# Linear attention and a two-layer network on one core: attention by head pairs, its divisor spread through DRAM, dense chunks of 512 tokens with attention pieces placed by hand

## The chip, the cores and the metric

The kernel runs on one core of a Trainium2 chip. The metric is the device time of one execution in microseconds (us), the median of several runs. A separate execution was taken by the profiler; its rows are what this document reads.

## The reference

```python
q, k, v: (8, 8, 576, 64)            # batch, heads, tokens, head size
phi = lambda x: np.where(x > 0, x, np.exp(x) - 1.0) + 1.0
q_p, k_p = phi(q), phi(k)
kv = np.einsum('bhsd,bhse->bhde', k_p, v)
z = np.sum(k_p, axis=2)
num = np.einsum('bhsd,bhde->bhse', q_p, kv)
den = np.einsum('bhsd,bhd->bhs', q_p, z)[..., None] + 1e-06
x = (num / den).transpose(0, 2, 1, 3).reshape(4608, 512)
h = x @ w_in                        # w_in: (512, 2048)
out = (h - np.tanh(h)) @ w_out      # w_out: (2048, 512)
```

## The kernel before, in words

A batch is 576 tokens, handled as four tiles of 128 tokens and one of 64, with tokens on the partitions. For each batch GpSimd queues the loads of q, k and v by token tile (they cast f32 to bf16 on the way, lines 96 to 98), behind the two weight loads that stand at the start of the program. `phi` makes each tile in three ScalarE steps (relu, exp, relu) and an addition on VectorE.

Then comes a loop over the eight heads. TensorE sums `kvz_ps` over the five tiles (line 114; column 65 of v is one, so it also sums k) and transposes q into `qTp` (line 117), which VectorE copies into `qT`. For each token tile TensorE makes `nd_ps`, numerator and divisor side by side (line 125); VectorE takes the reciprocal of the divisor, one value for each token, that is for each partition (line 127); ScalarE scales the numerator by it into `res` (line 129); TensorE transposes `res` into `resT` (line 131), and VectorE copies that into `xT_sb`, the feature-major input of the dense layers (line 132). The four PSUM tiles of attention have one buffer each.

After its heads a batch goes through `moe_chunk` twice, for 512 and for 64 tokens. The first layer makes `hps` for 128 of the 2048 features at a time, four matmuls each (line 72); ScalarE takes the tanh, VectorE the difference `gT` (lines 76, 77). The second layer makes `ops` for 128 tokens, 16 matmuls of 512 columns (line 82); VectorE copies it to `osb`, and SyncE writes it out.

The order of the instructions on each engine is decided by a scheduler, which takes from several heads and from both layers by priority; each engine then runs its own queue in order, and waits at an instruction until the tiles that it needs are there.

## Time and profile before

| | |
|---|---|
| median of 3 runs | 747.39 us (745.71 to 749.91) |
| the profiled execution, span from first to last instruction | 748.1 us |
| TensorE matmul busy | 556.6 us, 74% of the span, 2944 matmuls |
| VectorE, ScalarE busy | 346.5 us, 321.6 us |
| mean granted TensorE clock | 0.776 |

The page gives the profiled execution by its span alone; no time outside the span is known for it. Busy times of different engines overlap, so they don't add up to the span. The granted clock is given as a share of 2.4 GHz; the records know the levels 0.5 and 1.0 only, and a mean between them is a mixture. For the first 140 us or so the rows show 1.00 also where matmuls took the time of the lower level, so there the duration of matmuls is the better sign.

### The profile page before, as it was taken

To read this page: it belongs to the slowest core of one execution; us is meant where nothing else is said; L and a number is where in the kernel's file an instruction comes from. 1 tells how busy PE (TensorE), PEld (TensorE's weight loads), DVE (VectorE), ACT (ScalarE), POOL (GpSimd) and SP (SyncE) were. 2 spreads that over 40 slices of the span, in tenths; PEclk is the share of its full clock that TensorE was granted. 3 is DMA by queue.
4 is the path that set the end of the run, shared out by engine and by line. 5 is a ranking of instruction groups with operands and counts; after the bars stand their busy time and mean duration, and the time that the engine had idled before them with its cause. 6 is when DMAs were issued, how large, how long until landed. Compare 5 with 4: busy or idle time off the path is not lost.

```text
span 748.1 us, 9055 instructions
## 1 busy us (share of the span) xinstructions
PE 556.6 (74%) x2944; PEld 270.7 (36%) x2944; DVE 346.5 (46%) x1400; ACT 321.6 (43%) x817; POOL 107.6 (14%) x168
## 2 busy tenths in 40 slices
PE   0065689856997579965898569985699668985697
...
PEclk9999999855797559955698557975599656985599
...
DMA packets 120400, 28.38 MB, mean 38 GB/s; under 512 B 113184, under 2 KB 115232, under 8 KB 120352
## 3 DMA queue, kind: packets, MB, share of 16 engines
...
## 4 chain that ended last, share of the span: by engine, by line
PE 45%; issue 27%; ACT 10%; DVE 9%; DMA 4%; POOL 3%; POOLq 0%; ACTq 0%; DVEq 0%
PE hps L72 16%; PE ops L82 15%; PE resT L131 5%; PE qTp L117 4%; ACT res L129 4%; DMA v<-in_v_dram 4%; DVE xT_sb L132 3%; DVE rden L127 3%; PE kvz_ps L114 3%; ACT tmp L62 2%; ACT tmp L63 2%; DVE qT L118 2%; ACT qa L64 2%; PE nd_ps L125 2%; POOL v L98 1%
## 5 line engine op out<-in xcount | busy, mean ns | idle before, releaser
L72 PE MATMUL hps<-xT_sb,w_in_sb 128*128 128x64 bf16 (+1 forms) x1024 | 186.7, 314 | 7.0 <-DVE gT L77 3.1
L76 ACT ACTIVATE th<-hps 128x512 f32<-128x512 f32 (+1 forms) x256 | 103.8, 412 | 197.0 <-PE hps L72 187.5
L129 ACT ACTIVATE res<-nd_ps,rden 128x64 bf16<-128x64 f32 (+1 forms) x320 | 99.7, 311 | 198.7 <-DVE rden L127 198.5
L82 PE MATMUL ops<-w_out_sb,gT 128*128 128x512 bf16 (+1 forms) x640 | 173.3, 389 | 0.0
L77 DVE TENSOR_TENSOR gT<-hps,th 128x512 bf16<-128x512 f32 (+1 forms) x256 | 115.5, 456 | 105.5 <-ACT th L76 102.0
L131 PE MATMUL resT<-ident,res 128*64 128x128 bf16 (+1 forms) x320 | 92.2, 288 | 78.6 <-ACT res L129 74.8
L117 PE MATMUL qTp<-ident,qp 128*64 128x128 bf16 (+1 forms) x320 | 85.9, 268 | 81.2 <-DVE qT L118 44.4
L132 DVE COPY xT_sb<-resT 64x128 bf16<-64x128 bf16 (+1 forms) x320 | 67.0, 209 | 136.5 <-PE resT L131 133.1
L72 PEld LDWEIGHTS <-w_in_sb 128*128 128x128 bf16 x1024 | 75.1, 100 | 94.5 <-issue 46.4
L131 PEld LDWEIGHTS <-res 128*64 128x64 bf16 (+1 forms) x320 | 39.6, 124 | 170.9 <-ACT res L129 160.8
L98 POOL DMA_DIRECT2D v<-in_v_dram x40 | 33.8, 856 | 449.7 <-PE kvz_ps L114 446.4
L118 DVE COPY qT<-qTp 64x128 bf16<-64x128 bf16 (+1 forms) x320 | 65.0, 203 | 55.1 <-PE qTp L117 52.9
L82 PEld LDWEIGHTS <-gT 128*128 128x128 bf16 (+1 forms) x640 | 63.0, 101 | 71.2 <-DVE gT L77 6.2
L125 PE MATMUL nd_ps<-kvz,qT 64*128 64x65 bf16 (+1 forms) x320 | 74.2, 232 | 0.1
L117 PEld LDWEIGHTS <-qp 128*64 128x64 bf16 (+1 forms) x320 | 37.5, 125 | 72.8 <-DVE qp L65 36.7
L114 PE MATMUL kvz_ps<-v,kp 128*64 128x65 bf16 (+1 forms) x320 | 42.7, 241 | 20.5 <-POOL v L99 17.4
L127 DVE RECIPROCAL rden<-nd_ps 128x1 f32<-128x1 f32 (+1 forms) x320 | 52.7, 165 | 9.5 <-PE nd_ps L125 1.8
L85 DVE COPY osb<-ops 128x512 f32<-128x512 f32 (+1 forms) x40 | 27.6, 690 | 53.8 <-PE ops L82 53.4
L63 ACT ACTIVATE tmp<-tmp 128x512 bf16<-128x512 bf16 (+1 forms) x80 | 49.8, 622 | 0.0
L125 PEld LDWEIGHTS <-qT 64*128 64x128 bf16 (+1 forms) x320 | 33.1, 104 | 37.2 <-issue 8.6
L114 PEld LDWEIGHTS <-kp 128*64 128x64 bf16 (+1 forms) x320 | 30.7, 142 | 26.5 <-DMA v<-in_v_dram 13.1
...
## 6 DMA issues: line engine op xcount, KB each, us to landing
out_dram<-osb SPq DMA_DIRECT2D x32, 256.0 KB, 2.0
qa<-in_q_dram POOLq DMA_DIRECT2D x32, 128.0 KB, 4.1
ka<-in_k_dram POOLq DMA_DIRECT2D x32, 128.0 KB, 4.2
v<-in_v_dram POOLq DMA_DIRECT2D x32, 128.0 KB, 4.6
w_in_sb<-in_moe_w_in_dram POOLq DMA_DIRECT2D x1, 2048.0 KB, 12.8
w_out_sb<-in_moe_w_out_dram POOLq DMA_DIRECT2D x1, 2048.0 KB, 22.2
out_dram<-osb SPq DMA_DIRECT2D x8, 128.0 KB, 2.3
...
```

What stands on the lines that cost most here:

```text
L72: nc.tensor.matmul(hps, w_in_sb[:, kc, fi * 128:(fi + 1) * 128], xT_sb[:, kc, mo:mo + MC], start=(kc == 0), stop=(kc == KD - 1))
L76: nc.scalar.activation(th, hps, AF.Tanh)
L77: nc.vector.tensor_sub(gT[:, fi, :], hps, th)
L82: nc.tensor.matmul(ops, gT[:, fi, ms:ms + mw], w_out_sb[:, fi, :], start=(fi == 0), stop=(fi == n_ff - 1))
L114: nc.tensor.matmul(kvz_ps, kps[i][:, h, :], v1s[i][:, h, :], start=(i == 0), stop=(i == NT - 1))
L117: nc.tensor.transpose(qTp, qps[i][:, h, :], ident[:st, :st])
L118: nc.vector.tensor_copy(qT[:, so:so + st], qTp)
L125: nc.tensor.matmul(nd_ps, qT[:, so:so + st], kvz, start=True, stop=True)
L127: nc.vector.reciprocal(rden, nd_ps[:, 64:65])
L129: nc.scalar.activation(res, nd_ps[:, :64], AF.Copy, scale=rden)
L131: nc.tensor.transpose(resT, res, ident[:st, :st])
L132: nc.vector.tensor_copy(xT_sb[po:po + 64, pb, b * S + so: b * S + so + st], resT)
```

## The change

Attention works on pairs of heads, with features on the partitions. Of a batch the first 512 tokens are loaded as 128 partitions of four neighbouring tokens (`km`, `qm`, `vm`), the last 64 apart (`kraw`, `qraw`, `vr`). `phi` is now min(exp(x), max(x, 0) + 1): exp on ScalarE, the other two steps on VectorE, one instruction for all eight heads. Its tile `e` has two buffers. `a_kv` multiplies a pair's k by a pair's v and a block of ones; a mask keeps the diagonal blocks, so that `kz` holds for a pair a block-diagonal matrix of 128 columns, and the sums of k in columns 128 to 160. `a_qT` transposes q for a pair. `a_den` makes all divisors of a batch at once, with tokens on the free axis: VectorE adds 1e-6 and takes the reciprocal on 128 x 144 values, SyncE writes them to DRAM (`ds`) in four pieces and reads them back with each head's row repeated on 64 partitions (`rdb`). `a_num` makes the numerators feature-major, and VectorE multiplies them by `rdb` straight into `xT`, so that no result is transposed.

The dense layers take nine chunks of 512 tokens; a chunk spans two batches, and odd batches put their 64 remaining tokens first so that the columns fit. The order is now the program's own. Chunk 0 follows attention of batch 0 alone and runs its second layer in four quarters; attention of batch 1 follows alone. From chunk 1 on, pieces of the next batches' attention stand between groups of four matmuls: `s1` places them after a group of the first layer, `s2` after a group of the second. So chunk c holds `a_kv`, `a_den` and `a_num` of batch c + 1, and `phi` and `a_qT` of batch c + 2. Chunk 1 also holds `phi` and `a_qT` of batch 2. Weights are loaded in quarters, behind the loads of batch 0, and the output copy moves to ScalarE.

```diff
-    attn_ps = ctx.enter_context(tc.tile_pool(name="attn_ps", bufs=1, space=bass.MemoryType.PSUM))
-    mps = ctx.enter_context(tc.tile_pool(name="mps", bufs=2, space=bass.MemoryType.PSUM))
...
+    kpool = ctx.enter_context(tc.tile_pool(name="kpool", bufs=2))
+    work = ctx.enter_context(tc.tile_pool(name="work", bufs=2))
+    gpool = ctx.enter_context(tc.tile_pool(name="gpool", bufs=1))
+    mpool = ctx.enter_context(tc.tile_pool(name="mpool", bufs=3))
+    rpool = ctx.enter_context(tc.tile_pool(name="rpool", bufs=2))
+    dram = ctx.enter_context(tc.tile_pool(name="dram", bufs=2, space=bass.MemoryType.DRAM))
+    dps = ctx.enter_context(tc.tile_pool(name="dps", bufs=6, space=bass.MemoryType.PSUM))
+    aps = ctx.enter_context(tc.tile_pool(name="aps", bufs=2, space=bass.MemoryType.PSUM))
+    ctx.enter_context(tc.manual_schedule())
...
+    def col0(b):
+        return (S * b, S * b + SM) if b % 2 == 0 else (S * b + SR, S * b)
...
+    km_t, krr_t, qm_t, qrr_t = {}, {}, {}, {}
+    def load_k(b):
+        km = kpool.tile([128, H, J, D], BF16, name="km")
+        nc.gpsimd.dma_start(out=km.rearrange("p h j d -> p h (j d)"),
+                            in_=k[b, :, 0:SM, :].rearrange("h (p j) d -> p h (j d)", j=J))
+        kr = kpool.tile([SR, H, D], BF16, name="kraw")
+        nc.gpsimd.dma_start(out=kr, in_=k[b, :, SM:S, :].rearrange("h s d -> s h d"))
+        km_t[b], krr_t[b] = km, kr
+    def load_v(b):
+        vm, vr = vm_b[b % 2], vr_b[b % 2]
+        for p in range(NP):
+            nc.gpsimd.dma_start(
+                out=vm[:, p, 0:2].rearrange("p h j d -> p h (j d)"),
+                in_=v[b, 2 * p:2 * p + 2, 0:SM, :].rearrange("h (p j) d -> p h (j d)", j=J))
...
+    def phi(src, dst):
+        rows, n = src.shape[0], src.shape[1]
+        e = work.tile([128, H, J, D], BF16, name="e")
+        r = work.tile([128, H, J, D], BF16, name="r")
+        ev, rv = (e, r) if len(src.shape) == 4 else (e[0:rows, :, 0, :], r[0:rows, :, 0, :])
+        nc.scalar.activation(ev, src, AF.Exp)
+        nc.vector.tensor_scalar(rv, src, 0.0, 1.0, ALU.max, ALU.add)
+        nc.vector.tensor_tensor(dst, ev, rv, ALU.min)
+    def a_phi(b, main, rem, persist, store, name):
+        d = work.tile([128, J, H, D], BF16, name=name)
+        phi(main[b], d.rearrange("p j h d -> p h j d"))
+        phi(rem[b], persist[b % 2][0:SR])
...
+    def a_qT(b, p):
+        if p == 0:
+            qT_t[b] = work.tile([128, NP, S], BF16, name="qT")
+        qp, qr = qpm_t[b], qr_b[b % 2]
+        ps = aps.tile([128, 1024], BF16, name="tps", tag="aps")
+        for j in range(J):
+            nc.tensor.transpose(ps[:, j * 128:(j + 1) * 128], qp[:, j, 2 * p:2 * p + 2, :], ident)
+        nc.tensor.transpose(ps[:, SM:SM + 128], qr[:, 2 * p:2 * p + 2, :], ident)
+        nc.scalar.copy(qT_t[b][:, p, :], ps[:, 0:S])
+    def a_kv(b, half):
+        if half == 0:
+            kz_t[b] = work.tile([128, NP, 160], BF16, name="kz")
+        kp, kr, vm, vr = kpm_t[b], kr_b[b % 2], vm_b[b % 2], vr_b[b % 2]
+        ps = aps.tile([128, 2, 192], F32, name="kvps", tag="aps")
+        for i in range(2):
+            p = 2 * half + i
+            for j in range(J):
+                nc.tensor.matmul(ps[:, i, :], kp[:, j, 2 * p:2 * p + 2, :], vm[:, p, :, j, :],
+                                 start=(j == 0), stop=False)
+            nc.tensor.matmul(ps[:, i, :], kr[:, 2 * p:2 * p + 2, :], vr[:, p, :, :],
+                             start=False, stop=True)
+        nc.vector.tensor_mul(kz_t[b][:, 2 * half:2 * half + 2, :], ps[:, :, 0:160],
+                             mask[:, 2 * half:2 * half + 2, :])
+    def a_den(b):
+        kz, qT = kz_t[b], qT_t[b]
+        w = S // 4
+        ps = aps.tile([128, w], F32, name="denps", tag="aps")
+        for p in range(NP):
+            for j in range(4):
+                nc.tensor.matmul(ps[32 * j:32 * j + 32, :], kz[:, p, 128:160],
+                                 qT[:, p, j * w:(j + 1) * w], start=(p == 0), stop=(p == NP - 1))
+        den = rpool.tile([128, w], F32, name="den")
+        nc.vector.tensor_scalar(den, ps, 1e-6, None, ALU.add)
+        rden = rpool.tile([128, w], F32, name="rden")
+        nc.vector.reciprocal(rden, den)
+        ds = dram.tile([H, S], F32, name="ds")
+        for j in range(4):
+            nc.sync.dma_start(out=ds[:, j * w:(j + 1) * w], in_=rden[32 * j:32 * j + H, :])
+        rdb = rpool.tile([128, NP, S], F32, name="rdb")
+        for hh in range(2):
+            nc.sync.dma_start(
+                out=rdb[64 * hh:64 * hh + 64],
+                in_=ds[4 * hh:4 * hh + 4, :].partition_broadcast(64))
+        rdb_t[b] = rdb
+    def a_num(b, p):
+        kz, qT, rdb = kz_t[b], qT_t[b], rdb_t[b]
+        cm, cr = col0(b)
+        ps = aps.tile([128, 512], F32, name="numps", tag="aps")
+        if p < NP:
+            nc.tensor.matmul(ps, kz[:, p, 0:128], qT[:, p, 0:SM], start=True, stop=True)
+            nc.vector.tensor_mul(xT[:, p, cm:cm + SM], ps, rdb[:, p, 0:SM])
+        else:
+            pv = ps[:, 0:NP * SR].rearrange("p (a t) -> p a t", a=NP)
+            for i in range(NP):
+                nc.tensor.matmul(pv[:, i, :], kz[:, i, 0:128], qT[:, i, SM:S], start=True, stop=True)
+            nc.vector.tensor_mul(xT[:, :, cr:cr + SR], pv, rdb[:, :, SM:S])
...
+    def l1(c, fi, gT):
+        h = dps.tile([128, 512], F32, name="h", tag="dps")
+        for p in range(NP):
+            nc.tensor.matmul(h, w_in_sb[:, p, fi * 128:(fi + 1) * 128], xT[:, p, c * 512:(c + 1) * 512],
+                             start=(p == 0), stop=(p == NP - 1))
+        th = mpool.tile([128, 512], F32, name="th")
+        nc.scalar.activation(th, h, AF.Tanh)
+        nc.vector.tensor_sub(gT[:, fi, :], h, th)
+    def l2mm(gT, o, i, f0, f1):
+        for fi in range(f0, f1):
+            nc.tensor.matmul(o, gT[:, fi, i * 128:(i + 1) * 128], w_out_sb[:, fi, :],
+                             start=(fi == 0), stop=(fi == NF - 1))
+    def evac(c, i, o):
+        osb = mpool.tile([128, DM], F32, name="osb")
+        nc.scalar.copy(osb, o)
+        for rows, dst in out_rows(4 * c + i):
+            nc.sync.dma_start(out=dst, in_=osb[rows])
+    def new_o():
+        return dps.tile([128, 512], F32, name="o", tag="dps")
...
+    load_k(0)
+    load_v(0)
+    load_q(0)
+    for g in range(4):
+        load_w(g)
+    for g in range(4):
+        load_wo(g)
+    load_k(1)
...
+    def attention(b):
+        a_kphi(b)
+        a_kv(b, 0)
+        a_kv(b, 1)
+        a_qphi(b)
+        for p in range(NP):
+            a_qT(b, p)
+        a_den(b)
+        for p in range(NP + 1):
+            a_num(b, p)
+    attention(0)
+    load_k(2)
+    load_v(2)
+    load_q(2)
+    for c in range(NC):
+        gT = gpool.tile([128, NF, 512], BF16, name="gT")
+        n1, n2 = c + 1, c + 2
+        s1 = {i: [] for i in range(16)}
+        s2 = {i: [] for i in range(16)}
+        if c == 1 and n1 < B:
+            s1[0].append(lambda: a_kphi(n1))
+            s1[1].append(lambda: (a_qphi(n1), load_k(4), load_q(4)))
+            for p in range(NP):
+                s1[2 + 2 * p].append(lambda p=p: a_qT(n1, p))
+        if 1 <= c and n1 < B:
+            s1[9].append(lambda: a_kv(n1, 0))
+            s1[11].append(lambda: a_kv(n1, 1))
+            s1[13].append(lambda: a_den(n1))
+            for p in range(NP + 1):
+                s2[9 + p].append(lambda p=p: a_num(n1, p))
+        if 1 <= c and n2 < B:
+            s2[0].append(lambda: a_kphi(n2))
+            s2[1].append(lambda: a_qphi(n2))
+            for p in range(NP):
+                s2[3 + p].append(lambda p=p: a_qT(n2, p))
+        if c >= 1 and c + 3 < B:
+            s1[11].append(lambda: load_v(c + 3))
+        if c >= 1 and c + 4 < B:
+            s2[2].append(lambda: (load_k(c + 4), load_q(c + 4)))
+        if c == 0:
+            os_ = None
+            for g in range(4):
+                for fi in range(4 * g, 4 * g + 4):
+                    l1(c, fi, gT)
+                if os_ is None:
+                    os_ = [new_o() for _ in range(4)]
+                for i in range(4):
+                    l2mm(gT, os_[i], i, 4 * g, 4 * g + 4)
+            for i in range(4):
+                evac(c, i, os_[i])
+            for s in range(16):
+                for f in s2[s]:
+                    f()
+            attention(1)
+            load_k(3)
+            load_v(3)
+            load_q(3)
+            continue
+        for fi in range(NF):
+            l1(c, fi, gT)
+            for f in s1[fi]:
+                f()
+        for s in range(16):
+            i = s // 4
+            if s % 4 == 0:
+                o = new_o()
+            l2mm(gT, o, i, 4 * (s % 4), 4 * (s % 4) + 4)
+            if s % 4 == 3:
+                evac(c, i, o)
+            for f in s2[s]:
+                f()
```

On ScalarE, in the second half of a batch's dense work, the kernel before has tanh of the 64-token chunk mixed with `res` of the next batch:

```order
L76 ACTIVATE th<-hps 128x64 [waits PE_49,Activation_49] x2
L76 ACTIVATE th<-hps 128x64 [waits DVE_49,PE_49]
L129 ACTIVATE res<-nd_ps,rden 128x64 [waits DVE_49]
L76 ACTIVATE th<-hps 128x64 [waits PE_49,Activation_49] x2
L76 ACTIVATE th<-hps 128x64 [waits DVE_49,PE_49] x3
L129 ACTIVATE res<-nd_ps,rden 128x64 [waits DVE_49] x3
```

In the changed kernel the same place in chunk 2 (tanh of the first layer, then the second layer's half) reads as follows; `km`, `kraw`, `qm` and `qraw` are the loaded k and q of batch 4, `tps` the transposed q:

```order
L205 ACTIVATE th<-h 128x512 [waits DVE_49,PE_49] x13
L113 ACTIVATE e<-km 128x2048 [waits DMASW0_49]
L113 ACTIVATE e<-kraw 64x8x64 [waits DMASW1_49]
L113 ACTIVATE e<-qm 128x2048 [waits DMASW2_49,DVE_49]
L113 ACTIVATE e<-qraw 64x8x64 [waits DMASW3_49,DVE_49]
L215 COPY osb<-o 128x512 [waits DMAHW0_49,PE_49]
L137 COPY qT<-tps 128x576 [waits PE_49] x4
L215 COPY osb<-o 128x512 [waits DMAHW1_49,PE_49]
```

The small `res` are gone from the queue; four exponentials of another batch stand ahead of the output copies, and those on q wait for VectorE, which frees the tile `e`.

On TensorE the kernel before runs, where its first dense matmuls stand, attention and dense layers in turn:

```order
L131 LDWEIGHTS res
L131 MATMUL resT<-ident,res 64x128
L125 LDWEIGHTS qT
L125 MATMUL nd_ps<-kvz,qT 128x65
L72 LDWEIGHTS w_in_sb
L72 MATMUL hps<-xT_sb,w_in_sb 128x512
```

In the changed kernel, behind the fourth group of the second layer in chunk 2, TensorE has the transposes of batch 4's q (`qp` for the 512 tokens, `qr_94` for the 64), and then the fifth group:

```order
L135 LDWEIGHTS qp [waits DVE_49]
L135 MATMUL tps<-ident,qp 128x128 [waits PE_49]
...
L136 LDWEIGHTS qr_94 [waits DVE_49]
L136 MATMUL tps<-ident,qr_94 128x128
L210 LDWEIGHTS gT
L210 MATMUL o<-w_out_sb,gT 128x512
```

The second layer's matmuls of the same chunk stand behind transposes that wait for VectorE.

On SyncE the queue of the kernel before holds nothing but outputs:

```order
L86 DMA out_dram<-osb 128x512 [waits DVE_49] x4
L86 DMA out_dram<-osb 64x512 [waits DVE_49]
L86 DMA out_dram<-osb 128x512 [waits DVE_49] x3
L86 DMA out_dram<-osb 128x512 [waits DMAHW0_49,DVE_49]
L86 DMA out_dram<-osb 64x512 [waits DMAHW1_49,DVE_49]
```

In the changed kernel, for chunk 1, it holds the divisors' writes and reads, then the outputs:

```order
L168 DMA ds<-rden 8x144 [waits DMAHW0_49,DVE_49]
L168 DMA ds<-rden 8x144 [waits DMAHW1_49]
L168 DMA ds<-rden 8x144 x2
L171 DMA rdb<-ds 64x2304 [waits DMAHW2_49,DMAHW3_49,DMAHW1_49,DMAHW0_49]
L171 DMA rdb<-ds 64x2304
L217 DMA out_dram<-osb 64x512 [waits DMAHW6_49,Activation_49]
```

The reads wait until the writes have landed, and the outputs stand behind both.

## Rows read from the trace of the kernel before

**Rows 1.** The page's busy times and its clock in 40 slices.

```profile
PE 556.6 (74%) x2944; PEld 270.7 (36%) x2944; DVE 346.5 (46%) x1400; ACT 321.6 (43%) x817; POOL 107.6 (14%) x168
...
PEclk9999999855797559955698557975599656985599
```

**Rows 2.** Stretches: length, engines' busy time, clock, DMA share, GB/s.

```profile
142.00:190.00 48.00, 30.37 (x150) 15.90 (x149) 24.03 (x123) 26.69 (x67) 13.11 (x20) 0.52 0.60 40
194.00:219.00 25.00, 25.00 (x113) 10.72 (x111) 11.07 (x16) 7.78 (x13) 0.00 (x0) 0.97 0.09 32
219.00:230.00 11.00, 10.80 (x101) 5.84 (x99) 5.98 (x32) 4.54 (x21) 0.00 (x0) 1.00 0.07 26
230.00:278.00 48.00, 29.95 (x149) 15.73 (x148) 23.82 (x122) 26.48 (x67) 13.10 (x20) 0.53 0.60 40
```

**Rows 3.** The waits: us in total, times, longest.

```profile
ACT res L129 <- DVE rden L127: 198.5, 207, 4.1
...
PEld L131 <- ACT res L129: 160.8, 226, 1.0
```

**Rows 4.** A stretch of the dense stage, TensorE alone: busy time and matmuls.

```profile
200.00:218.00 18.00, 18.00 (x84) 1.00 0.11 40
```

**Rows 5.** Timeline of TensorE: start, length, merged matmuls; two dense starts, four short ones.

```profile
103.46 3.40 PE L72 MATMUL hps<-xT_sb,w_in_sb 128*128 128x512 bf16 x8
...
190.47 3.57 PE L72 MATMUL hps<-xT_sb,w_in_sb 128*128 128x512 bf16 x8
193.84 1.48 PE L82 MATMUL ops<-w_out_sb,gT 128*128 128x512 bf16 x3
...
738.32 0.29 PE L72 MATMUL hps<-xT_sb,w_in_sb 128*128 128x64 bf16 x4
```

**Rows 6.** Groups by shape: count, busy us, mean ns, idle before and its cause.

```profile
L77 DVE TENSOR_TENSOR gT<-hps,th 128x512 bf16<-128x512 f32 x128 | 87.7, 690 | 74.1 <-ACT th L76 73.6
...
L76 ACT ACTIVATE th<-hps 128x512 f32<-128x512 f32 x128 | 75.7, 598 | 78.8 <-PE hps L72 77.8
...
L127 DVE RECIPROCAL rden<-nd_ps 128x1 f32<-128x1 f32 x256 | 42.6, 166 | 7.2 <-PE nd_ps L125 1.4
...
L63 ACT ACTIVATE tmp<-tmp 128x512 bf16<-128x512 bf16 x64 | 39.9, 624 | 0.0
...
L76 ACT ACTIVATE th<-hps 128x64 f32<-128x64 f32 x128 | 28.1, 225 | 118.2 <-PE hps L72 109.7 <-DVE rden L127 5.6 <-DVE gT L77 1.9
L77 DVE TENSOR_TENSOR gT<-hps,th 128x64 bf16<-128x64 f32 x128 | 27.8, 223 | 31.4 <-ACT th L76 28.4
...
L65 DVE TENSOR_TENSOR qp<-qa,tmp 128x512 bf16<-128x512 bf16 x32 | 13.3, 416 | 35.3 <-ACT qa L64 35.3
```

**Rows 7.** DMA issues: count, KB each, median us from issue to landing.

```profile
out_dram<-osb SPq DMA_DIRECT2D x32, 256.0 KB, 2.0
qa<-in_q_dram POOLq DMA_DIRECT2D x32, 128.0 KB, 4.1
...
w_out_sb<-in_moe_w_out_dram POOLq DMA_DIRECT2D x1, 2048.0 KB, 22.2
```

**Rows 8.** Timeline of GpSimd at the start: start, length, what it issues.

```profile
1.27 0.90 POOL L40 DMA_DIRECT2D w_in_sb<-in_moe_w_in_dram  x1 [0.33 <-issue]
...
2.49 1.18 POOL L42 DMA_DIRECT2D w_out_sb<-in_moe_w_out_dram  x1
3.66 0.90 POOL L96 DMA_DIRECT2D qa<-in_q_dram  x1
```

**Rows 9.** The output line: duration of an issue in ns, landing time in us.

```profile
L86 SPq DMA_DIRECT2D out_dram<-osb x40: 332/333/542, 124.1 to 744.8; - x40
...
DMA to landing us min/median/max: 2.0/2.0/3.6
```

**Rows 10.** Timeline of the end: the last matmuls, the last copy.

```profile
743.23 0.81 PE L82 MATMUL ops<-w_out_sb,gT 128*64 128x512 bf16 x2
...
744.08 0.68 DVE L85 COPY osb<-ops 64x512 f32<-64x512 f32 x1 [0.49 <-PE ops L82]
```

More of the change, by code (lines that the diff above doesn't have):

```diff
@@ L11 @@
 AF = mybir.ActivationFunctionType
+ALU = mybir.AluOpType
 @with_exitstack
@@ L29 @@
     DF = moe_w_in.shape[1]
-    KD = DM // 128
-    n_ff = DF // 128
-    const = ctx.enter_context(tc.tile_pool(name="const", bufs=1))
-    ident = const.tile([128, 128], BF16)
-    make_identity(nc, ident)
-    xT_sb = const.tile([128, KD, N], BF16, name="xT_sb")
-    wpool = ctx.enter_context(tc.tile_pool(name="wpool", bufs=1))
-    w_in_sb = wpool.tile([128, KD, DF], BF16)
-    nc.gpsimd.dma_start(out=w_in_sb, in_=moe_w_in.rearrange("(ko ki) f -> ki ko f", ki=128))
-    w_out_sb = wpool.tile([128, n_ff, DM], BF16)
@@ L67, in moe_chunk @@
-    def moe_chunk(mo, MC):
-        gT = gpool.tile([128, n_ff, MC], BF16, name="gT")
-        for fi in range(n_ff):
-            hps = mps.tile([128, MC], F32, name="hps")
-            for kc in range(KD):
-                nc.tensor.matmul(hps, w_in_sb[:, kc, fi * 128:(fi + 1) * 128],
-                                 xT_sb[:, kc, mo:mo + MC],
-                                 start=(kc == 0), stop=(kc == KD - 1))
-            th = mpool.tile([128, MC], F32, name="th")
-            nc.scalar.activation(th, hps, AF.Tanh)
-            nc.vector.tensor_sub(gT[:, fi, :], hps, th)
-        for ms in range(0, MC, 128):
-            mw = min(128, MC - ms)
-            ops = mps2.tile([mw, DM], F32, name="ops")
-            for fi in range(n_ff):
-                nc.tensor.matmul(ops, gT[:, fi, ms:ms + mw], w_out_sb[:, fi, :],
-                                 start=(fi == 0), stop=(fi == n_ff - 1))
-            osb = mpool.tile([mw, DM], F32, name="osb")
-            nc.vector.tensor_copy(osb, ops)
-            nc.sync.dma_start(out=out[mo + ms: mo + ms + mw, :], in_=osb)
@@ new lines @@
+    w_out_sb = const.tile([128, NF, DM], BF16, name="w_out_sb")
+    vm_b = [const.tile([128, NP, 3, J, D], BF16, name=f"vm{i}") for i in range(2)]
+    vr_b = [const.tile([128, NP, 3, D], BF16, name=f"vr{i}") for i in range(2)]
+    kr_b = [const.tile([128, H, D], BF16, name=f"kr{i}") for i in range(2)]
+    qr_b = [const.tile([128, H, D], BF16, name=f"qr{i}") for i in range(2)]
+    def col0(b):
+        return (S * b, S * b + SM) if b % 2 == 0 else (S * b + SR, S * b)
+    km_t, krr_t, qm_t, qrr_t = {}, {}, {}, {}
@@ new lines, in load_k @@
+    def load_k(b):
[12 more added lines that the diff above has]
+        for p in range(NP):
+            nc.gpsimd.dma_start(
+                out=vr[0:SR, p, 0:2, :],
+                in_=v[b, 2 * p:2 * p + 2, SM:S, :].rearrange("h s d -> s h d"))
@@ new lines, in load_q, with load_w @@
+    def load_q(b):
+        qm = kpool.tile([128, H, J, D], BF16, name="qm")
+        nc.gpsimd.dma_start(out=qm.rearrange("p h j d -> p h (j d)"),
+                            in_=q[b, :, 0:SM, :].rearrange("h (p j) d -> p h (j d)", j=J))
+        qr = kpool.tile([SR, H, D], BF16, name="qraw")
+        nc.gpsimd.dma_start(out=qr, in_=q[b, :, SM:S, :].rearrange("h s d -> s h d"))
+        qm_t[b], qrr_t[b] = qm, qr
+    def load_w(g):
+        f0 = g * (DF // 4)
+        nc.gpsimd.dma_start(out=w_in_sb[:, :, f0:f0 + DF // 4],
+                            in_=moe_w_in[:, f0:f0 + DF // 4].rearrange("(ko ki) f -> ki ko f", ki=128))
@@ new lines @@
+    make_identity(nc, ident)
+    load_k(0)
[6 more added lines that the diff above has]
+    load_k(1)
+    load_v(1)
+    load_q(1)
+    nc.vector.memset(mask, 0.0)
+    for hh in range(2):
+        nc.vector.memset(mask[64 * hh:64 * hh + 64, :, 64 * hh:64 * hh + 64], 1.0)
+        for p in range(NP):
+            m = 128 + 4 * hh + p
+            nc.vector.memset(mask[64 * hh:64 * hh + 64, p, m:m + 1], 1.0)
+    for i in range(2):
+        nc.vector.memset(vr_b[i][64:128], 0.0)
+        nc.vector.memset(kr_b[i][64:128], 0.0)
+        nc.vector.memset(qr_b[i][64:128], 0.0)
+        nc.vector.memset(vm_b[i][:, :, 2], 1.0)
+        nc.vector.memset(vr_b[i][0:SR, :, 2], 1.0)
```

94 lines of the change are left out of this document (28 added, 66 removed).

## The prediction

> **What bounds the kernel now.** I read the page's totals first, then the stages, then the waits. TensorE is busy 74% of the span, at a granted clock that swings between its two levels, 1.2 and 2.4 GHz [rows 1]. The windows by stage show why. Each batch has about 48 us in which TensorE runs 150 short matmuls, is idle over a third of the time and sits at a clock of 0.52 (attention), and about 36 us in which it is full at a clock of 1.0 (the dense layers) [rows 2]. The waits name the sparse stage's cause: ScalarE's `res` waits for VectorE's reciprocal, and TensorE's next transpose for `res`, hundreds of times [rows 3]. So a round trip of small operations through three engines bounds attention, and TensorE's rate bounds the rest. From 142 to 230 us, one batch, are 88 us; eight of them and the loading ahead of the first make the 748.1 us span. The page gives no time outside the span; the median, 747.39, is 0.1% from it, so I sum to the span. Changes under 0.5% could not be told from none.
>
> **The dense matmuls.** Chunks of 512 and 64 tokens become nine of 512: 9 x 128 = 1152 matmuls of 512 columns. At full clock 84 matmuls filled 18 us [rows 4]: 0.214 us each, 27.4 us a chunk. A start from a rest costs more: one dense stage began with eight matmuls in 3.40 us, another with eight in 3.57 and three more in 1.48 [rows 5], so 3.4 to 4.7 us at half rate, 1.7 to 2.4 lost. I take 2.0 for each start.
>
> **Attention on TensorE.** For a batch 160 + 160 small matmuls become 20 transposes of 128 columns, 20 of 192, 16 of 144, four of 512 and four of 64: 11,008 columns. The rate is 0.42 ns a column for long matmuls [rows 4]; four of 64 columns took 0.29 us, most of it one latency, a pitch of 0.03 us, 0.47 ns a column [rows 5]. With 0.45: 4.9 us, and 3.8 us where a chunk has no transposes. The operations `res`, `rden`, `resT` and their copies go: the waits of [rows 3] go with them.
>
> **VectorE and ScalarE beside a chunk.** Tanh 0.598 us x 16, four output copies at the same price and 4 copies of 576 elements near 0.65 make 14.6 us of ScalarE; two elu's exponentials add 5. Sixteen subtractions at 0.690 us are 11.0 of VectorE, five multiplications of the numerator 3.2, the elu about 6 [rows 6]. Both stay near 21 us under TensorE's 32: no engine but TensorE bounds by its sum. The order on the engines is another matter.
>
> **Where phi is late.** The queues run in program order. In a chunk's second half TensorE meets `qT`'s transposes after four groups, 16 x 0.214 = 3.4 us in, and they need `qp`. ScalarE starts the exponentials only after the last tanh, 0.75 us in. A 512-element one takes 0.624, and 0.833 ns more per element (0.598 against 0.225 us, for 512 and 64) give 1.90 us for 2048 [rows 6]. So exp k ends at 2.65. VectorE's minimum: 0.416 us for 512; with the fixed 0.156 that the two subtractions give (0.690 and 0.223), 1.20 for 2048 [rows 6]. It ends at 4.0. The tile `e` has two buffers, both taken by k, so exp q runs from 4.1 to 6.0; its minimum ends at 7.35, the 64-row remainder at 8.05. TensorE therefore waits about 4.5 us, and whatever stands behind the transposes, 12 groups of the second layer, waits with it. I add 2.0 for the clock. `tensor_scalar` (max, add) is nowhere in the trace: below, nothing, since exp covers it up to about 1.2 us; above, at the f32 subtraction's slope, 2.3 us, 2 us more per chunk. I take the lower, as the bf16 row is nearer. In chunk 1 phi of batch 2 also lies in the first half; by the same chain TensorE stands from 2.6 to 8.9 us there, 6.3 + 2.0.
>
> **The denominator's way through DRAM.** Per batch: add and reciprocal on 128 x 144 (reciprocal between 0.3 us, the 0.166 row plus a nanosecond an element, and 1.4 at eight times that rate; I take 0.7), four writes, two reads of 0.59 MB each. SyncE issues at 0.33 us and an output lands after 2.0 to 3.6 [rows 9]: writes 1.0 + 2.3. For 1.18 MB the nearest rows are the weights: 4.19 MB of bf16 (8.39 MB read) had landed 24.7 us into the span, the first issue at 1.27 [rows 7, 8]: 179 GB/s by what is written, 358 by what is read. So 3.3 to 6.6 us and 2.0 of latency; beside loads up to twice. I take 8.6 alone, 12.3 beside loads. From the end of the denominator's matmuls that is 13 to 16.6 us. In chunks 1 to 5 TensorE reaches the third numerator 17.9 us after them (two groups, ten slots, four transposes, and phi's wait): hidden, and no longer so if that wait goes. Behind SyncE's wait stand only output DMAs. In chunk 6, without phi, the cover is 12.1 us: 2 us wait.
>
> **The parts laid bare.** Attention 0 and 1 have no dense work beside them. GpSimd now issues k, eight pieces of v, then q: at 0.9 us each [rows 8], q is issued at 10.4 us and, 1.77 MB at 179 GB/s and 4.1 us from issue to landing [rows 7], is here at about 15.6. Then exp 1.9, minimum and remainder 1.9, transposes and four copies 3.2, denominator matmuls, add, reciprocal 2.5, writes 3.3, read 12.3, multiplications 3.2: chunk 0 starts at 44 us. Chunk 0 holds four `o` tiles of the six PSUM buffers, so `h` has two: a pair of groups takes 0.86 + 0.60 + 0.69 and hand-overs, 2.46 us, where TensorE needs 1.72; with the wait for the last `gT` I put 6.7 us on its four quarters: 27.4 + 2 + 6.7 = 36.1, to 80.1. Attention 1 follows serially: output copies 1.0, the phi chain 7.3, then the same tail, 32.5: chunk 1 starts at 112.6.
>
> **The sum.** Chunk 1: 27.4 + 4.9 + 2.0 + 8.3 + 6.5 = 49.2, to 161.8. Chunks 2 to 5: 27.4 + 4.9 + 4.5 + 2.0 = 38.8 each, to 317. Chunk 6: 27.4 + 3.8 + 2 = 33.2, to 350. Chunks 7 and 8: 54.8, to 405. After the last matmul the old kernel needs 4.1 us [rows 10]: 409 us.
>
> **The rivals.**
> - TensorE doesn't wait for phi. Against it, exp q's wait for a buffer; for it, that all pieces are bounded by estimates. Then 5 x 6.5 + 8.3 us go: 368 us, and up to 383 if the reads' 16.6 us then stand out against 13.4 of cover. Chance 0.17.
> - VectorE's `tensor_scalar` waits for GpSimd's issues. k's tile is reloaded just when phi has read it, so an issue of 0.9 us can stand ahead of q's `tensor_scalar`. Priced: three such waits in each of six phi stages and four in the bare ones, 2.7 x 6 + 3.6 = 20 us: 429 us. For it, the timing; against it, that the old bf16 `tensor_tensor`, which ran beside GpSimd's issues too, has a mean of 0.416 [rows 6]. Chance 0.10. The Trainium skill, "SBUF — State Buffer", section "Who interferes with whom", states that a VectorE operation in a two-port mode, which `tensor_scalar` can enter and `tensor_tensor` cannot, and GpSimd shut each other out for a whole instruction. By that rule this rival's time holds; the trace has no such pair of operations.
> - The broadcast read is slow, say 25 us: 64 partitions read one row. Attention 0 and 1 take 13 more each, chunks 1 to 5 11.4 each, chunk 6 17: 509 us. Nothing in the trace reads one row 64 times. Chance 0.07.
> - The dense chunks stay at the lower clock: 1152 x (0.427 - 0.214) = 245 us, less the starts' 18: 636 us. Full stages all rose to 1.0 within 5 us [rows 2, 5]. Chance 0.03.
> - Slower than before: the broadcast alone, if a round trip costs more than its cover by (748 - 409) / 8 = 42 us, thus from about 55 us on, 21 GB/s for 1.18 MB; at 60 us, 8 x 5 us over that, 790 us. Even the old loads with their 128 KB pieces moved 40 GB/s over whole stages in which they rested half the time [rows 2]. Chance 0.01.
>
> **How the numbers follow.** My forecast has 0.62. Its own range, from tensor_scalar's two bounds (+12), the reads (-11 to +13), starts and the bare parts, is 385 to 435. The range 360 to 450 takes in the first two rivals and leaves out the last three and some of each edge, under 2 in 10. Only the last case is not faster by over 0.5%; I give 0.98, 0.01, 0.01.
>
> **What would show it.** In the new profile: chunks 2 to 5 with a period near 39 us; one TensorE wait of 4 to 5 us on VectorE's `qp` in the second half of chunks 1 to 5 and a clock that falls after it; dense matmuls at 0.214 us; `rdb` landing 7 to 13 us after its issue, with no wait for it but in attention 0, 1 and chunk 6; chunk 0's first matmul near 44 us, chunk 1's near 113. Wrong would be: no wait for `qp`, a wait for `rdb` in every chunk, dense stages at a clock of 0.5, or first matmuls off by over 15 us.

## The result, and the profile after

The changed kernel takes 398.4 us (median of four, 397.2 to 398.9) against 748.3 for the kernel before (745.7 to 749.9, now four runs): a ratio of 0.533, 95% interval 0.531 to 0.535. The forecast was 409 us, own range 385 to 435. The profiled execution has a span of 396.2 us, and by that the steps are compared below. Every run takes 1.7 to 1.9 us more than its span from first to last instruction; the forecast, which summed to the span, left this out.

The page's busy times and TensorE's clock in 40 slices, after:

```profile
PE 310.3 (78%) x1664; PEld 148.3 (37%) x1664; DVE 184.6 (47%) x301; ACT 165.3 (42%) x245; POOL 75.1 (19%) x110
...
PEclk9855799965569989998998999899989999999999
```

TensorE's share is little higher than in [rows 1], but its busy time has fallen by 246 us, with 1664 matmuls for 2944. VectorE and ScalarE have lost about half of theirs. The clock is low where attention 0 and 1 stand alone and in the first matmuls of chunks 0 and 1 behind them (slices 2 to 5 and 9 to 12), and dips once more in each chunk from 1 to 5.

The waits of the new kernel (us in total, times, longest):

```profile
DVE xT L182 <- DMA rdb<-ds: 35.6, 3, 15.9
...
PE numps L181 <- DVE xT L182: 29.6, 3, 17.1
PE tps L135 <- DVE qp L115: 28.8, 8, 4.5
...
PE kvps L147 <- DVE kp L115: 15.5, 2, 10.7
```

The hundreds of short waits of [rows 3] are gone. Three stand in their place: for `qp` in all eight phi chains (attention 0 and 1, both halves of chunk 1, the second halves of chunks 2 to 5), for the read `rdb` three times only, for `kp` where attention stands alone. The timeline shows where:

```profile
23.73 1.40 SPq L168 DMA_DIRECT2D ds<-rden  x4
29.02 1.17 SPq L171 DMA_DIRECT2D rdb<-ds  x2
...
40.33 1.18 PE L181 MATMUL numps<-qT,kz 128*128 128x512 bf16 x2 [17.07 <-DVE xT L182]
...
41.88 2.75 PE L202 MATMUL h<-xT,w_in_sb 128*128 128x512 bf16 x6
...
53.77 1.89 PE L202 MATMUL h<-xT,w_in_sb 128*128 128x512 bf16 x8 [0.55 <-DVE gT L206]
...
93.51 1.30 SPq L168 DMA_DIRECT2D ds<-rden  x4
95.87 1.09 SPq L171 DMA_DIRECT2D rdb<-ds  x2
...
104.47 1.18 PE L181 MATMUL numps<-qT,kz 128*128 128x512 bf16 x2 [11.43 <-DVE xT L182]
...
106.76 1.86 PE L202 MATMUL h<-xT,w_in_sb 128*128 128x512 bf16 x4 [0.56 <-DVE xT L187]
...
115.62 0.61 PE L135 MATMUL tps<-ident,qp 128*128 128x128 bf16 x4 [4.53 <-DVE qp L115]
...
133.18 1.90 ACT L113 ACTIVATE e<-km 128x2048 bf16<-128x2048 bf16 x1
...
135.11 1.22 DVE L115 TENSOR_TENSOR kp<-e,r 128x2048 bf16<-128x2048 bf16 x1 [0.27 <-ACT e L113]
...
136.37 1.91 ACT L113 ACTIVATE e<-qm 128x2048 bf16<-128x2048 bf16 x1 [0.78 <-DVE kp L115]
...
138.31 1.22 DVE L115 TENSOR_TENSOR qp<-e,r 128x2048 bf16<-128x2048 bf16 x1 [0.66 <-ACT e L113]
...
139.59 0.40 PE L135 MATMUL tps<-ident,qp 128*128 128x128 bf16 x4 [3.49 <-DVE qp L115]
140.31 0.23 PE L136 MATMUL tps<-ident,qr 128*128 128x128 bf16 x1 [0.32 <-DVE qr L115]
140.38 1.58 PE L210 MATMUL o<-w_out_sb,gT 128*128 128x512 bf16 x4
...
142.29 1.91 PE L210 MATMUL o<-w_out_sb,gT 128*128 128x512 bf16 x4
...
144.34 1.03 PE L210 MATMUL o<-w_out_sb,gT 128*128 128x512 bf16 x4
...
177.28 0.40 PE L135 MATMUL tps<-ident,qp 128*128 128x128 bf16 x4 [3.50 <-DVE qp L115]
...
332.80 0.38 PE L181 MATMUL numps<-qT,kz 128*128 128x512 bf16 x1 [1.05 <-DVE xT L182]
```

Read chunk 1's second half from 133.18: exp of k, k's minimum, only then exp of q (its release is VectorE's `kp`, which frees a buffer of `e`), q's minimum, and TensorE's transposes 3.49 us late. The two groups of four behind it take 1.58 and 1.91 us where a group at full clock shows 1.03. From 177.28 the same comes again 37.7 us later.

Windows of the same execution: the stretch after that wait and most of the rest of the period (us, busy of TensorE and of the other engines, clock, DMA share, GB/s):

```profile
140.00:145.00 5.00, 4.69 (x23) 2.37 (x24) 0.26 (x1) 1.74 (x3) 0.68 (x1) 0.66 1.17 210
145.00:177.00 32.00, 28.78 (x167) 13.94 (x165) 20.12 (x31) 17.34 (x26) 7.74 (x11) 1.00 0.51 85
```

Groups by shape, the answer to [rows 6]:

```profile
L113 ACT ACTIVATE e<-qm 128x2048 bf16<-128x2048 bf16 x8 | 15.3, 1910 | 10.1 <-DMA qm<-in_q_dram 5.1 <-DVE kp L115 5.0
...
L115 DVE TENSOR_TENSOR qp<-e,r 128x2048 bf16<-128x2048 bf16 x8 | 9.8, 1225 | 4.8 <-ACT e L113 4.6
...
L165 DVE RECIPROCAL rden<-den 128x144 f32<-128x144 f32 x8 | 8.4, 1053 | 0.3
```

### The profile page after: what moved, and what is told of

It reads as the page before. It is cut to its first block, busy times and chain, and to the rows that moved or that the text cites. A ratio compares the mean times of both kernels' runs of the same rounds, so it can differ in the third digit from the quotient of the medians.

```text
span 396.2 us, 4437 instructions
## 1 busy us (share of the span) xinstructions
PE 310.3 (78%) x1664; PEld 148.3 (37%) x1664; DVE 184.6 (47%) x301; ACT 165.3 (42%) x245; POOL 75.1 (19%) x110
## 3 DMA queue, kind: packets, MB, share of 16 engines
q0 software_dynamic: 42624, 18.36, 37.7%
## 4 chain that ended last, share of the span: by engine, by line
PE 65%; DMA 12%; DVE 10%; ACT 9%; issue 2%; SPq 1%; POOL 0%; DVEq 0%; ACTq 0%; POOLq 0%
PE h L202 31%; PE o L210 25%; ACT e L113 6%; DMA rdb<-ds 6%; PE kvps L147 3%; DVE qp L115 2%; DVE kp L115 2%; DMA ds<-rden 2%; PE tps L135 2%; PE numps L181 2%; DMA km<-in_k_dram 2%; DMA qm<-in_q_dram 2%; DVE gT L206 1%; ACT th L205 1%; DVE xT L182 1%
## 5 line engine op out<-in xcount | busy, mean ns | idle before, releaser
L210 PE MATMUL o<-w_out_sb,gT 128*128 128x512 bf16 x576 | 142.7, 394 | 2.4 <-DVE gT L206 1.9
L202 PE MATMUL h<-xT,w_in_sb 128*128 128x512 bf16 x576 | 135.3, 389 | 2.2 <-DVE gT L206 1.6
L206 DVE TENSOR_TENSOR gT<-h,th 128x512 bf16<-128x512 f32 x144 | 98.6, 688 | 80.9 <-ACT th L205 80.9
L205 ACT ACTIVATE th<-h 128x512 f32<-128x512 f32 x144 | 86.0, 597 | 105.7 <-PE h L202 101.3
L210 PEld LDWEIGHTS <-gT 128*128 128x128 bf16 x576 | 56.5, 101 | 69.9 <-issue 6.2
L182 DVE TENSOR_TENSOR xT<-numps,rdb 128x512 bf16<-128x512 f32 x32 | 21.6, 690 | 83.0 <-PE numps L181 47.2
L215 ACT COPY osb<-o 128x512 f32<-128x512 f32 x36 | 21.0, 583 | 74.7 <-PE o L210 73.4
L79 POOL DMA_DIRECT2D vm<-in_v_dram x32 | 22.6, 719 | 89.3 <-PE kvps L147 81.7
L137 ACT COPY qT<-tps 128x576 bf16<-128x576 bf16 x32 | 20.0, 639 | 30.9 <-PE tps L136 30.9
L135 PEld LDWEIGHTS <-qp 128*128 128x128 bf16 x128 | 11.5, 117 | 40.3 <-DVE qp L115 32.5
L83 POOL DMA_DIRECT2D vr<-in_v_dram x32 | 19.3, 623 | 14.4 <-DMA w_out_sb<-in_moe_w_out_dram 8.5
L113 ACT ACTIVATE e<-qm 128x2048 bf16<-128x2048 bf16 x8 | 15.3, 1910 | 10.1 <-DMA qm<-in_q_dram 5.1
## 6 DMA issues: line engine op xcount, KB each, us to landing
w_in_sb<-in_moe_w_in_dram POOLq DMA_DIRECT2D x4, 512.0 KB, 10.1
```

Source lines behind the costliest of these rows:

```text
L79: nc.gpsimd.dma_start(out=vm[:, p, 0:2].rearrange("p h j d -> p h (j d)"), in_=v[b, 2 * p:2 * p + 2, 0:SM, :].rearrange("h (p j) d -> p h ...
L113: nc.scalar.activation(ev, src, AF.Exp)
L135: nc.tensor.transpose(ps[:, j * 128:(j + 1) * 128], qp[:, j, 2 * p:2 * p + 2, :], ident)
L182: nc.vector.tensor_mul(xT[:, p, cm:cm + SM], ps, rdb[:, p, 0:SM])
L202: nc.tensor.matmul(h, w_in_sb[:, p, fi * 128:(fi + 1) * 128], xT[:, p, c * 512:(c + 1) * 512], start=(p == 0), stop=(p == NP - 1))
L205: nc.scalar.activation(th, h, AF.Tanh)
```

## The experiments

The theory: TensorE's rate sets the time, and what lies above it are three exposed chains: phi ahead of the transposes, the divisor's way through DRAM, and attention 0 and 1 bare. The rivals: a smaller cause in the same places (buffer, clock, contention), or a dense part with no room for the pieces.

**A third buffer for `e`** (all runs change the new kernel).

```diff
-        e = work.tile([128, H, J, D], BF16, name="e")
+        e = epool.tile([128, H, J, D], BF16, name="e")      # epool: bufs=3
```

> The tile e of phi gets a third buffer, so the exponential of q need not wait for VectorE's minimum on k. Theory (TensorE stands at the transposes because phi's chain ends late, and each microsecond of that chain counts): exp q starts about 0.8 us earlier, the minimum on q about 0.65, in five chunks' second halves, in chunk 1's first half and in the two bare attentions: 4 to 6 us less, 392 to 395 us, and a wait of 2.8 us instead of 3.5. Rival (the time is held by something behind the wait, the reads of the divisor): the wait shortens and the time stays at 398.

Measured: 393.0 us (392.8 to 394.1). In the timeline (lines are one further down) the wait is still there:

```profile
138.33 0.40 PE L136 MATMUL tps<-ident,qp 128*128 128x128 bf16 x4 [2.95 <-DVE qp L116]
```

2.95 us for 3.49: the buffer is a part of the wait, and the longer one is the chain itself, two exponentials of 1.9 us and a minimum of 1.2 behind the last tanh.

**Matmuls into the wait**, to split the stall from the clock.

```diff
+            s2[3].append(fill)      # 20 unread matmuls of 512 columns
             for p in range(NP):
                 s2[3 + p].append(lambda p=p: a_qT(n2, p))
```

> Ahead of the transposes that wait for phi in the second halves of chunks 1 to 5, TensorE runs 20 matmuls of 512 columns whose result nobody reads (4.3 us, about the length of the wait). The wait is filled, not shortened. Theory (after the wait TensorE runs at the lower clock, which costs about 2 us each time): five times 2 us less, and 0.4 us of overhang each: about 390 us, with a granted clock of 1.0 after the wait. Rival (the slow matmuls after the wait have another cause): 398 to 401 us, and the matmuls after the fill still take 0.43 us.

Measured: 391.2 us (391.0 to 391.9), though each fill lasts longer than the wait:

```profile
136.64 4.48 PE L222 MATMUL fillps<-xT,w_in_sb 128*128 128x512 bf16 x20
140.96 0.39 PE L135 MATMUL tps<-ident,qp 128*128 128x128 bf16 x4
...
142.38 1.03 PE L210 MATMUL o<-w_out_sb,gT 128*128 128x512 bf16 x4
```

The fill holds the transposes up for 4.32 us (136.64 to 140.96); without it they stood for 3.65 (135.94, where the fill would have started, to 139.59) and 0.32 more for `qr`. So each fill is 0.35 us longer than the wait that it covers, and yet the kernel is 7.2 us faster, since the groups behind it run at 1.03 us: (7.2 + 5 x 0.35) / 5 = 1.8 us a chunk belong to the clock alone. The timeline of the kernel without the fill gives 1.7: two groups with their transposes from 140.38 to 144.34, 3.96 us, where the next takes 1.14 (to 145.48).

**The transposes five groups later.**

```diff
-                s2[3 + p].append(lambda p=p: a_qT(n2, p))
+                s2[8 + p].append(lambda p=p: a_qT(n2, p))
```

> The transposes of q move from behind groups 4 to 7 of the second layer to behind groups 9 to 12, among the numerators, so that phi has 3.4 us of cover more than it needs. Theory: the wait of 3.8 us and the 2 us of lower clock go in five chunks, 29 us, and the reads of the divisor then stand out by 0 to 4 us in chunks 1 to 3 (loads beside them) and by about 1 us in chunks 4 and 5, as they do in chunk 6: 370 to 384 us. Rival (the reads take the whole place of the wait): 395 us or more, with waits for rdb of 4 to 6 us in each chunk.

Measured: 381.2 us (379.2 to 383.8), 17.2 less. The wait for `qp` is gone from the second halves, and another stands there, as the forecast's cover of 13.4 us without phi's wait had it:

```profile
179.60 0.38 PE L135 MATMUL tps<-ident,qp 128*128 128x128 bf16 x4 [3.16 <-DVE xT L182]
...
179.88 1.03 PE L210 MATMUL o<-w_out_sb,gT 128*128 128x512 bf16 x4
```

`xT` waits for `rdb`: in the changed kernel the read came in time only because TensorE had stood still for phi. The group behind this stop takes 1.03 us, and the granted clock from 179.6 to 184 is 1.00: a stop of 3.16 us cost no clock here, while one of 2.95 and 0.32 in the run with a third buffer did (the groups behind it take 1.52 and 1.91 us). What decides between the two isn't shown.

**No pieces in the chunks**: each batch's attention alone behind a chunk.

```diff
-        if 1 <= c and n1 < B:
+        if False:                # so too for phi, the transposes and the loads
...
+        if n1 < B:
+            attention(n1)        # behind the chunk, then the loads of batch c + 3
```

> No attention piece stands between matmul groups: attention of each batch follows a chunk alone, as that of batch 1 does, and the loads follow it. Theory (the new form alone leaves attention bound by its serial chain of about 30 us a batch; the placement hides it): 77 + 6 x (29.7 + 29.4) + 29.7 + 29.4 + 27.4 and the tail, about 520 us (505 to 530), so that of the 350 us gained about 228 belong to the new form and 120 to the placement. Rival (the new form is what gains, and the placement hides little): 430 to 450 us.

Measured: 519.0 us (518.1 to 520.0), ratio to before 0.693 [0.691, 0.696]. The wait for the numerator's multiplication, which waits for `rdb`:

```profile
PE numps L181 <- DVE xT L182: 100.0, 8, 17.5
```

So everything but the placement (the new form, the equal chunks, the weights in quarters) gives 229 us of the 350 (748.3 - 519.0), and laying attention into the chunks 121.

**No read of the divisors.**

```diff
-        for hh in range(2):
-            nc.sync.dma_start(out=rdb[64 * hh:64 * hh + 64],
-                in_=ds[4 * hh:4 * hh + 4, :].partition_broadcast(64))
-        rdb_t[b] = rdb
+        rdb_t[b] = rdb_c         # a constant tile of ones
```

> The two reads of the eight denominator rows are left out and every multiplication takes a constant tile of ones, so that the division is not computed; the matmuls, the addition, the reciprocal and the four small writes stay. My theory: the round trip through DRAM costs only where no dense matmuls stand in front of its first user. The changed kernel shows TensorE waiting for it 17.1 us in attention 0, 11.4 us in attention 1 and 1.1 us in chunk 6, and not at all in chunks 1 to 5. Without it: 398.4 - 29.6 = 369 us, range 364 to 378 (its upper part if in chunk 0 the weights, which were being loaded during the wait, are late next). In chunks 1 to 5 the period of a chunk stays at 37.7 us and the wait for qp at 3.5 us. Rival 1, that the wait in attention 0 only covers the loads of the two weight matrices: chunk 0 then waits for them, and 382 to 388 us. Rival 2, that the reads also slow the chunks (their 1.18 MB on the same DMA engines as the next batch's k and q, their multiplications on VectorE): the period of chunks 2 to 5 falls by 1 us or more each, and the time is below 364 us.

Measured: 370.7 us (369.5 to 372.9). Chunk 0 starts at 26.18 instead of 41.88 and meets no wait for weights, and the wait and the period of chunks 1 to 5 are the old ones to a few hundredths:

```profile
26.18 4.39 PE L197 MATMUL h<-xT,w_in_sb 128*128 128x512 bf16 x15 [0.22 <-issue]
...
150.22 0.40 PE L135 MATMUL tps<-ident,qp 128*128 128x128 bf16 x4 [3.50 <-DVE qp L115]
...
187.91 0.40 PE L135 MATMUL tps<-ident,qp 128*128 128x128 bf16 x4 [3.50 <-DVE qp L115]
```

The way through DRAM costs 27.7 us by the medians. By the two profiled executions it is 15.7 us in attention 0, 10.4 in attention 1, 1.05 in chunk 6 and 0.8 in chunk 0's first quarter; in chunks 1 to 5 it is free. Both rivals fall.

**Attention 1 inside chunk 0.**

```diff
+            s0[0].append(lambda: a_kphi(1))
+            s0[4].append(lambda: a_qphi(1))
...                               # kv at 5 and 7, transposes at 7 and 8
+            s0[9].append(lambda: a_den(1))
+            for p in range(NP + 1):
+                s0[14 if p < 3 else 15].append(lambda p=p: a_num(1, p))
...
-            attention(1)
```

> The parts of attention 1 are placed between the second-layer groups of chunk 0 instead of behind it; nothing else changes. My theory: what stood alone cost 29.7 us, of which TensorE's own work is 4.9 us; the rest were waits (4.75 us for kp, 2.7 us for qp, 11.4 us for the read) that dense matmuls now cover. 398.4 - (29.7 - 4.9) = 373.6 us, range 370 to 382, the upper part if exp of k and q (2.5 us each on ScalarE), placed ahead of tanh of the next quarter, hold that quarter's first layer up, or if the read (8 to 10 us) outlasts the quarter in front of its first user. Rival, that most of those 29.7 us were transfers and vector work which chunk 0 cannot hide because its own quarters wait for VectorE already (0.5 us in each): 385 to 392 us.

Measured: 380.2 us (379.3 to 381.2): 18.2 us of the 24.8. The rest is one wait, read in the timeline:

```profile
71.56 1.34 SPq L168 DMA_DIRECT2D ds<-rden  x4
77.01 1.09 SPq L171 DMA_DIRECT2D rdb<-ds  x2
...
86.23 0.59 PE L181 MATMUL numps<-qT,kz 128*128 128x512 bf16 x1 [6.18 <-DVE xT L182]
```

From the last small write's issue to the read's 4.1 us go by, against 1.05 where attention 1 stood alone (94.81 to 95.87). GpSimd's loads of batch 3 now run at that time (issued from 59.5 to 72 us; the DMA engines are busy throughout from 72 to 77), since phi frees their buffers earlier.

**Later loads of k and q**, on top of the later transposes.

```diff
-            s2[2].append(lambda: (load_k(c + 4), load_q(c + 4)))
+            s2[14].append(lambda: (load_k(c + 4), load_q(c + 4)))
```

> The kernel with later transposes (381.2 us) plus one edit: k and q of batch c+4 are asked for after group 14 of the second layer instead of group 2, so that they do not run beside the read of the denominators. My theory: the 1 to 3.2 us that TensorE waits for the read in chunks 1 to 5 of that kernel (8.7 us in all) come from the loads beside it; without them the read takes about 8 us, the waits fall to 3 us or less in all, and with the clock that goes with them the time is 381.2 - 7 = 374 us (371 to 378). Rival, that the read is as long by itself: the waits stay, 380 to 383 us. Second rival, that k and q come too late for the next but one chunk: a wait of exp for km, and a time above 385 us.

Measured: 382.6 us (380.9 to 383.3), the same as without. But the edit had moved nothing, as GpSimd's and SyncE's timeline of chunk 2 shows:

```profile
170.29 0.92 POOL L70 DMA_DIRECT2D km<-in_k_dram  x1 [3.04 <-ACT e L113]
...
170.41 1.12 SPq L171 DMA_DIRECT2D rdb<-ds  x2
```

GpSimd has nothing but loads in its queue, and issues one as soon as its own wait is over, here for exp to have read `km`; where it stands in the program's text makes no difference. So this run tells nothing of the rival.

**The same, held back by a copy that needs `rdb`.**

```diff
-            s2[2].append(lambda: (load_k(c + 4), load_q(c + 4)))
+            s2[14].append(lambda: (nc.gpsimd.tensor_copy(junk, rdb_t[n1][:, 0, 0:1]),
+                                   load_k(c + 4), load_q(c + 4)))
```

> What the run with later loads meant to do: the kernel with later transposes (381.2 us), k and q of batch c+4 asked for in the order after group 14, and held on GpSimd by a copy of one column of this chunk's rdb, so that they cannot start before the read has landed (without it GpSimd asked for them as soon as their buffers were free, at the same moment as before). My theory: the read takes 8.1 us with no load beside it (chunks 4 and 5, which have none) and 9.9 to 10.2 in chunks 2 and 3, where km is asked for at the same moment; TensorE's waits for it fall from 3.2 and 2.5 us in chunks 2 and 3 to 1.0 to 1.2, as in chunks 4 and 5, and the time is 381.2 - 3.6, with up to 2 us of the clock: 376.5 us (374.5 to 379). Rival, that something else makes the reads of chunks 2 and 3 longer (the small rows of v just ahead): the waits stay above 2 us, 380 to 383 us.

Measured: 376.7 us (376.2 to 377.6), and the copy dates the landing:

```profile
169.61 1.12 SPq L171 DMA_DIRECT2D rdb<-ds  x2
...
177.87 0.18 POOL L288 COPY junk<-rdb 128x1 f32<-128x1 f32 x1 [11.42 <-DMA rdb<-ds]
...
178.58 0.38 PE L135 MATMUL tps<-ident,qp 128*128 128x128 bf16 x4 [1.32 <-DVE xT L182]
```

Issue to landing is 8.26 us with no load beside it, and TensorE's wait falls from 3.16 to 1.32. From the read's issue to the first multiplication it is 8.2 and 8.0 us in chunks 2 and 3, against 10.1 and 9.5 without the hold: a load asked for at the same moment lengthens the read by 1.5 to 1.9 us.

**The read of attention 0 ahead of the weights.**

```diff
+            nc.gpsimd.tensor_copy(junk, rdb_t[0][:, 0, 0:1])
+            for g in range(1, 4):
+                load_wo(g)       # then the loads of batch 1; both stood before attention 0
```

> The changed kernel with one edit: three of the four loads of the second weight matrix and the loads of batch 1 stand on GpSimd behind a copy of one column of attention 0's rdb, so that they start only when the read has landed. My theory: in attention 0 the round trip takes 15.8 us from the first small write (23.7) to the first multiplication (39.6), against 10.2 in attention 1 (93.5 to 103.7), because writes and reads share the DMA engines with the weights' loads. With these behind it the round trip takes 10 to 11 us, chunk 0 starts at 36 to 37 instead of 41.9, and the time is 398.4 - 5.3 = 393 us (391 to 396). Rival 1, that the weights come too late for chunk 0's second layer: TensorE waits there for w_out, and 396 to 402 us. Rival 2, that the round trip is no longer alone than beside loads: chunk 0 starts at 41 to 42, 397 to 400 us.

Measured: 394.4 us (394.4 to 396.6).

```profile
28.87 1.17 SPq L171 DMA_DIRECT2D rdb<-ds  x2
...
36.90 0.18 POOL L254 COPY junk<-rdb 128x1 f32<-128x1 f32 x1 [22.62 <-DMA rdb<-ds]
...
39.17 5.85 PE L202 MATMUL h<-xT,w_in_sb 128*128 128x512 bf16 x16
```

The read is back to 8.0 us, but cannot start sooner: the small writes still take 3.4 us to land beside what is being loaded. Chunk 0 starts 2.7 us earlier, not 5.3. Chunk 0's first quarter and attention 1 give half of that back in this execution, the slowest of the five (chunk 1 starts at 105.36, 1.4 earlier), so the 4 us between the medians are not fully placed: the time came out as expected, the mechanism by half.

**Everything covered**: later transposes, attention 1 in chunk 0, batch 2's transposes four groups later in chunk 1 (the later loads are in it too, in the form that moves nothing), and from chunk 2 on:

```diff
-            s1[9].append(lambda: a_kv(n1, 0))
-            s1[11].append(lambda: a_kv(n1, 1))
-            s1[13].append(lambda: a_den(n1))
+            s1[9 if c == 1 else 6].append(lambda: a_kv(n1, 0))
+            s1[11 if c == 1 else 8].append(lambda: a_kv(n1, 1))
+            s1[13 if c == 1 else 10].append(lambda: a_den(n1))
```

> Later transposes, later loads of k and q, attention 1 in chunk 0, in chunk 1 the transposes of batch 2 four groups later, and from chunk 2 on the key-value product and the denominators three groups earlier (2.6 us). My theory, that the time above dense work is waits for the phi chain and the read, and nothing else: 381.2 us with the later transposes, less 24.8 for attention 1, less 3.6 + 1 for the first half of chunk 1, less 8.7 with some 2 of the clock for the read: 381.2 - 40.1 = 341 us, range 336 to 352. TensorE's wait for qp and for xT then stands at under 1 us in any of chunks 1 to 5. Rival, that the waits move into the dense matmuls instead (VectorE and ScalarE late for tanh and gT, because the parts now press together): 352 to 368 us, with gT as the releaser.

Measured: 346.0 us (345.3 to 346.4), ratio to before 0.461 [0.460, 0.462]. Its window from 125 to 341 us, and a row of its timeline:

```profile
125.00:341.00 216.00, 213.95 (x1186) 104.38 (x1207) 122.09 (x190) 112.23 (x173) 22.34 (x32) 1.00 0.41 85
```

```profile
85.70 0.38 PE L181 MATMUL numps<-qT,kz 128*128 128x512 bf16 x1 [4.47 <-DVE xT L182]
```

TensorE is busy 99% of these 216 us, at full clock. Of the 5 us over the expected 341 most is the read in chunk 0; in chunk 1 a wait of 1.15 us for `xT` is left, where under 1 was expected. The waits did not move into the dense matmuls: the rival falls.

## Why the prediction was right, step by step

- **What bounds it.** Right. With every chain covered a chunk takes what its matmuls take (31.9 us in chunks 2 to 5 of the last run, 27.6 in chunk 7), and nothing else shows there.
- **Dense 27.4 us.** Chunks 7 and 8 run from 336.8 to 392.2: 27.7 each.
- **Attention on TensorE, 4.9 and 3.8 us.** 4.2 (31.9 - 27.7) and, from chunk 6's 31.9 us (304.9 to 336.8) less its 1.05 of wait, 3.2. A little high.
- **Phi's wait, 4.5 + 2.0 us.** 3.8 (3.49 and 0.32) + 1.7 to 1.8. The order was as told, exp q behind `e`'s buffer too; its links end up to 0.3 us sooner than worked out, the four transposes of `qp` (0.40 us) run before the 64-row remainder is there, and `tensor_scalar`, 0.68 us, stays within the 1.2 that exp hides. In chunk 1's first half 4.5 was measured for 6.3: the wait ends as forecast (115.62, for 106.76 + 8.9), but begins later, since the 12 matmuls ahead of it took 4.3 us at the lower clock for 2.6. That each stop costs some 2 us of clock came true in all five chunks, but it is no rule: the stop of 3.16 us in the run with later transposes cost none.
- **The read.** 7.8 to 8.4 us alone for an estimate of 8.6; beside loads, from issue to first multiplication, 10.6 in attention 0 for 12.3, a figure that stands in the prediction without a working. Hidden in chunks 1 to 5, 1.05 us of wait in chunk 6 (2 expected), and not hidden once phi's wait goes, as the cover said (its 17.9 us count twelve groups of the second layer, not the ten that the text names). The reciprocal is 1.05 us, not 0.7; the writes, 1.3 + 1.05 for 3.3, make up for it where no loads run. In attention 0 they take 5.3 (23.73 to 29.02).
- **The bare parts.** Chunk 0 starts at 41.9 (44), lasts 35.2, to 77.1 (36.1; the rows show 0.47 to 0.55 us for `gT` twice in a quarter, and the lower clock at its start), attention 1 takes 29.7 (32.5). That chunk 0's start is only 2 us off is in part luck: in attention 0 the writes are 2.0 us longer than priced, the read 1.7 and the multiplications 0.9 shorter.
- **The sum.** Start -2.1, chunk 0 -0.9, attention 1 -2.8, chunk 1 -1.7, chunks 2 to 5 -1.1 each, chunk 6 -1.3, chunks 7 and 8 +0.6 together: 409 becomes 396. All but the last have one sign; the 13 us are many estimates, most of them a little on the safe side, not one mechanism. Chunk 1's sum counts one set of transposes where two stand, 1 us too little, and its slow start twice, once as 2.0 us and once in a wait that is 1.8 too long; the second hides the first. The slow broadcast's 509 us count chunk 6's 2 us twice, and the old loads behind the 40 GB/s rested two fifths of the time, not half; neither bears on the forecast.

The rivals: no wait for phi was not the case here, and when it was made so (381) the reads stood out just as that rival's upper figure, 383, had it. VectorE's wait for GpSimd was priced at 20 us. Such pairs do occur, and they cost little. The group of `r` on q and of `kraw`'s issue (duration in ns: least, median, most), and a pair from chunk 1's second half:

```profile
L114 DVE TENSOR_SCALAR r<-qm x8: 675/677/894, 15.0 to 287.7; 128x2048 bf16<-128x2048 bf16 x8
...
L73 POOL DMA_DIRECT2D kraw<-in_k_dram x8: 681/768/1466, 2.4 to 212.4; - x8
...
136.98 0.68 DVE L114 TENSOR_SCALAR r<-qm 128x2048 bf16<-128x2048 bf16 x1
137.11 0.82 POOL L73 DMA_DIRECT2D kraw<-in_k_dram  x1
```

In the second halves of chunks 1 to 3 GpSimd issues `kraw` 0.1 us after `r` of q has begun: `r` keeps its 0.68 us, and the issue takes 0.82 to 0.86 us, for 0.68 to 0.72 where nothing runs beside it. Two pairs are longer. In attention 1, where GpSimd issues ten loads in a row, `r` of q takes 0.89 us; in chunk 1's first half an issue of `kraw` takes 1.47 us (from 113.04), with `r` of q starting in its middle (113.56) and taking its 0.68. By the rule of the Trainium skill, "SBUF — State Buffer", section "Who interferes with whom", either engine may shut the other out. That all of these lengthen agrees with it, and the issue of 1.47 us is longer by about the whole of `r`. But VectorE, whose wait the rival priced at 0.9 us each time, lost 0.2 us once. In sum it is 1.4 us of engine time.

The slow broadcast, the low clock and the side of "slower" fall with the read's 8 us and the window at 1.00.
